# Longformer attention and a cosine MLP on one core: values through a padded ring in DRAM, global rows through a scratch, and two waits fewer in the opening order

## The chip, the cores and the metric

One core of a Trainium2 chip runs the whole program. The metric is device time in microseconds (us). A core has a matrix engine (TensorE, PE; loading of its weights is shown as PEld), a vector engine (DVE), a scalar engine (ACT), GpSimd (POOL) and a sync engine (SP). Each takes its own instructions in order and waits on semaphores for the others. DMAs are issued here by SP (plain copies and transposes) and by POOL (copies that change the type, and indirect gathers); both kinds run on the same 16 DMA engines, from two queues (q1 for SP's, q0 for POOL's).

## The reference, cut to what matters

```python
# q, k, v: (8, 8, 576, 64) fp32; global_idx: 8 sorted positions
scores = scale * np.matmul(q, k.transpose(0, 1, 3, 2))
mask = np.abs(pos[:, None] - pos[None, :]) <= 32
mask = mask | is_global[:, None] | is_global[None, :]
scores = np.where(mask, scores, -1e9)
attn = np.exp(scores - scores.max(-1)) / (sum + 1e-9)
x = np.matmul(attn, v)            # then (8 * 576, 512): heads side by side
h = x @ w_in                      # 512 -> 2048
out = (h * np.cos(h)) @ w_out     # 2048 -> 512
```

## The kernel before

The 64 heads are worked in 32 **pairs** (two heads of one batch element); two pairs, four heads, are a **half** (16 halves, numbered like the steps s). A head's 576 rows are cut into 12 blocks of 48 queries. A block sees 112 keys (its 48 and 32 on either side) and the 8 global keys: KW = 120 rows. Before row 0 the window is filled with the head's own last 32 rows (KL = 32), after the last row with any finite rows; the mask takes out what does not count. The global queries ride as 8 extra columns in every block.

For one pair `pr` the steps are:
- `local_k`, `local_q` (k, q in the order strings): keys and queries of the blocks into `kw` and `qb`. Up to pair 7 they come from `kn`, `qn` (loaded by POOL, `load_qk`) and PE turns them; ACT copies, and L419, a small POOL copy, puts the last 32 keys in front. From pair 8 on they come from `kT`, `qT`, which SP loads with DMA transposes (`turn_half`, L262, L263) out of the fp16 copies `k16`, `q16` in DRAM; DVE copies (L423 to L437).
- `globals_kq` (g): POOL copies the global columns into `kw`, `qb` (L393 to L398).
- `scores` (s): 12 matmuls `st` (L447), ACT's exp (L449), DVE's mask (L450).
- `values` (p): 24 matmuls `pv` (L458) with the value tile `vw[pr % 4]`; DVE divides by the sums into `xn` (L463 to L469). `p5` is this step for pair 5.
- `turn_x` (x): PE turns `xn` (L481), DVE writes `xT` (L484); after a batch element's last pair POOL writes its 8 global rows (L489).

**Values.** `cast_half` with "v" (L246) has POOL copy four heads of v to fp16 in DRAM, `v16`, one array for all heads. `load_v` fills a pair's `vw` tile from it with four SP DMAs, or five for odd pairs: block 0 apart, its wrapped 32 rows apart, blocks 1 to 11 per head, and for odd pairs the last block of the second head apart. `load_vg` (L309) adds the 8 global value rows per head from `vgw`, an SBUF tile that `spread_globals` (ACT, L379) writes every eight pairs from the gathered rows `vg32`. Every window row is a run of 64 fp16, 128 bytes.

**Global rows.** For every eight pairs POOL gathers the global rows of k, q and v (L284); ACT copies k's and q's (`copy_globals`, L368), PE turns them (`turn_globals`, L373).

**MLP.** `mlp_in` (one, "1"): four matmuls `ph` (L497), ACT's cosine (L500), DVE's product (L501). `mlp_out` (two, "2"): four matmuls `po` (L511). They fill PE between attention steps as far as whole batch elements are ready. From pair 32 on only the MLP is left.

**Order.** The order is written out by hand: each engine runs its instructions in the order in which the code issues them. Pairs 0 to 3 and what feeds later ones follow the string `FRONT`; then a loop over s = 2 to 15 runs `THIRD` (s = 2) or `ORDER`, with scores of pair 2s (`sa`) and 2s+1 (`sz`), their values (`pa`, `pz`), and local keys for the next step (`kc` to `qd`). `G` calls `casts(s)`: POOL waits for pair 2s+1's `xn` with a small copy into `gate` (L680), then in s = 2, 6 and 10 gathers the next global rows, and casts a half of v, k, q (in s = 4 two). In the same steps `b` calls `copy_globals`, `t` `turn_globals` and `spread_globals`. At the end of a step SP issues `turn_half(s + 2)` and the loads of pairs 2s+4 and 2s+5.

In `FRONT`, besides the letters above: `I` loads the indices into POOL registers; `W0` to `W3` and `O0` to `O3` are POOL loads of quarters of w_in and w_out with a change of type; `L2` loads k and q of half 2 into `kn`, `qn`; `c2` casts v of half 2; `v4` is `load_values(4)` on SP; `n` a sum of squares on ACT. `w3` makes POOL wait until pair 3's values have landed, by a one-element copy out of `vw` (L660); `w5` and `w7` do the same for pairs 5 and 7. Everything that POOL has behind such a step in its order waits with it.

Of the kernel before, what the change touches and what calls it, by code (L numbers as in the profile page):

```python
# [10 lines left out]
FP16 = mybir.dt.float16  # L11
# [6 lines left out]
B, H, S, D = 8, 8, 576, 64  # L18
NT, DM, DFF = 4608, 512, 2048
P = 128  # L20
NP = H // 2
QB = 48
NB = 12
G = 8
W = 112
KW = G + W
BP = 6
GP = 8
KL = 32
# [11 lines left out]

THIRD = "sa0 sa1 sa2 sz0 sz1 sz2 1 pa 1 xa pz G 1 1 kc qc xz 1 1 b kd qd 1 n t 1"

FRONT = ("g0 k1 q1 s0.0 s0.1 s0.2 g1 s1.0 s1.1 s1.2 g2 g3 k2 q2 p0 s2.0 s2.1 s2.2 k3 q3 p1 x0 s3.0 s3.1 s3.2 I w3 W0 L2 W1 c2 c3 "
         "p2 x1 p3 x2 x3 g4 g5 v4 v5 1 1 k4 q4 w5 W2 L3 W3 1 1 k5 q5 n0 1 1 v6 v7 g6 g7 w7 O0 O1 O2 O3")
OK_ALL = float(P * (B * NP * 2 * BP + B))


def view(ap, *dims):

    return bass.AP(ap.tensor, ap.offset, [ap.ap[0], *[list(d) for d in dims]])


def dview(ap, offset, *dims):

    return bass.AP(ap.tensor, ap.offset + offset, [list(d) for d in dims])
# [134 lines left out]
def kernel(  # L191
# [10 lines left out]
    nc = tc.nc  # L202
# [3 lines left out]
    dram = ctx.enter_context(tc.tile_pool(name="dram", bufs=1, space=bass.MemoryType.DRAM))  # L206
# [18 lines left out]

    q16 = dram.tile([2 * B, S, 4 * D], FP16)
    k16 = dram.tile([2 * B, S, 4 * D], FP16)
    v16 = dram.tile([B * H * S, D], FP16)


    NV = 4
# [4 lines left out]
    vw = [keep.tile([P, 2, NB, D + 1], FP16, name=f"vw{i}") for i in range(NV)]  # L236
# [4 lines left out]
    def cast_half(s, which):  # L241

        base = s * 4 * S * D
        for x in which:
            if x == "v":
                nc.gpsimd.dma_start(v16[s * 4 * S : (s + 1) * 4 * S].rearrange("(n r) d -> n (r d)", r=16),  # L246
                                    dview(v, base, (16 * D, 4 * S // 16), (1, 16 * D)))
            else:
                src, dst = {"k": (k, k16), "q": (q, q16)}[x]
                nc.gpsimd.dma_start(dst[s].rearrange("t (h d) -> t h d", h=4),  # L250
                                    dview(src, base, (D, S), (S * D, 4), (1, D)))
# [8 lines left out]
    def turn_half(s):  # L260

        nc.sync.dma_start(kT[s % 2][:, :, KL : KL + S], k16[s], transpose=True)  # L262
        nc.sync.dma_start(qT[s % 2], q16[s], transpose=True)  # L263
# [24 lines left out]


    vgw = keep.tile([P, NB, D + 1], FP16)  # L290

    def load_v(pr):


        vt, n0, p0 = vw[pr % NV], 2 * pr * S * D, G + KL
        nc.sync.dma_start(vt[p0:KW, :, 0, 0:D], dview(v16, n0, (D, W - KL), (S * D, 2), (1, D)))
        nc.sync.dma_start(vt[G:p0, :, 0, 0:D], dview(v16, n0 + (S - KL) * D, (D, KL), (S * D, 2), (1, D)))
        for h in range(2):
            lo, i1 = n0 + (h * S - KL) * D, NB
            if pr % 2 and h:  # L300

                i1 = NB - 1
                nc.sync.dma_start(vt[G : KW - KL, h, i1, 0:D], dview(v16, lo + QB * i1 * D, (D, W - KL), (1, D)))  # L303
            nc.sync.dma_start(vt[G:KW, h, 1:i1, 0:D], dview(v16, lo + QB * D, (D, W), (QB * D, i1 - 1), (1, D)))

    def load_vg(pr):
        for h in range(2):
            p0 = (pr % GP * 2 + h) * G
            nc.sync.dma_start(vw[pr % NV][0:G, h], vgw[p0 : p0 + G])  # L309


    mask = keep.tile([KW, NB, 2, C], FP16)
# [52 lines left out]
    def copy_globals(which):  # L365
        for x in which:
            g16 = g16_of[x] = work.tile([P, 2, D], FP16, tag="g16", name="g16")
            nc.scalar.copy(g16, view({"k": kg32, "q": qg32}[x], (0, 2), (1, D)))  # L368

    def turn_globals(which, n):  # L370
        for x in which:
            t = ps.tile([P, GP, 2, G], FP16, tag="s", bufs=3)
            nc.tensor.transpose(t.rearrange("x n h g -> x (n h g)"), g16_of.pop(x).rearrange("x h d -> x (h d)"), ident16)  # L373
            for h in range(2):
                hp = slice(h * D, (h + 1) * D)
                nc.scalar.copy({"k": kgT, "q": qgT}[x][hp, GP * n : GP * (n + 1)], t[hp, :, h])

    def spread_globals():
        nc.scalar.copy(vgw[:, :, 0:D], view(vg32, (0, NB), (1, D)))  # L379


    w_in16 = const.tile([P, NC, DFF], FP16)
# [143 lines left out]
    def x_squares(s):  # L526

        sq = work.tile([P, 2 * BP * P], FP16, tag="sq", bufs=1)
        xn = xn_of.pop(s)
        nc.scalar.activation(sq, view(xn, (1, 2 * BP * P)), AF.Square,  # L530
                             accum_out=x_sq[:, s : s + 1])
# [47 lines left out]
    def one(n=1):  # L579
        for _ in range(n):  # L580

            if ins_q and ins_q[0][0] < ready[0] and ins_q[0][0] < outs_q[0][0] + 2:
                t, f = ins_q.pop(0)
                mlp_in(t, f)
                ready[1] = t * NF + f + 1

    def two(n=1):
        for _ in range(n):
            t, u = outs_q[0] if outs_q else (NTT, 0)

            need = min(t * NF + 4 * (u % 4) + 12, NTT * NF) if tail[0] else min(t * NF + 4 * (u % 4) + 7, (t + 1) * NF)
            if outs_q and need <= ready[1] and (tail[0] or NTT * NF - len(outs_q) < outs_by[0]):
                mlp_out(*outs_q.pop(0))
# [7 lines left out]
    with tc.manual_schedule():  # L601
# [16 lines left out]
        nc.gpsimd.iota(d_i, pattern=[[-1, C]], base=0, channel_multiplier=1)  # L618
        index_rows()
        for i in range(NV):  # L620
            if i % 2:
                nc.vector.memset(vw[i][:, 1, NB - 1], 0.0)
            nc.vector.memset(vw[i][:, :, :, D : D + 1], 1.0)
        gather(k, kg32, 0)
        gather(q, qg32, 0)
        cast_half(0, "v")
        cast_half(1, "v")
        gather(v, vg32, 0)
        load_qk(1)
# [7 lines left out]
        local_q(0)  # L637
        nc.vector.memset(view(pv[:, :, D : D + 1], (512, 2), (65, 6)), 1.0)
        load_v(0)
        spread_globals()  # L640
        load_vg(0)
        for pr in (1, 2, 3):
            load_v(pr)
            load_vg(pr)

        def load_w_in(c):
            nc.gpsimd.dma_start(w_in16[:, :, c * 512 : (c + 1) * 512],
                                moe_w_in[:, c * 512 : (c + 1) * 512].rearrange("(c p) n -> p c n", p=P))
# [5 lines left out]
        def load_values(pr):  # L654
            load_v(pr)
            load_vg(pr)
# [17 lines left out]
        def globals_kq(pr):  # L674
            globals_k(pr)
            globals_q(pr)

        def casts(s):

            nc.gpsimd.tensor_copy(gate[0:1], xn_of[s][0:1, 1, 0, 0:1])  # L680
            if s % 4 == 2 and s // 4 < 3:
                for src, dst in ((k, kg32), (q, qg32), (v, vg32)):
                    gather(src, dst, s // 4 + 1)
            for n in range(4, 2 * B):
                if s == (n - 2 if n < 7 else n - 3):
                    cast_half(n, "vkq")
# [4 lines left out]
                 "I": load_idx, "O": load_w_out, "w": wait_values, "1": units}  # L691
        for step in FRONT.split():
            f = (STEPS | OTHER)[step[0]]
# [5 lines left out]
        for s in range(2, B * NP // 2):  # L699
            outs_by[0] = 4 * (s - 2) if s < 5 else 8 * (s - 3)  # L700
            for pr in (2 * s + 2, 2 * s + 3):
                if 8 <= pr < B * NP:
                    globals_kq(pr)
            for step in (THIRD if s == 2 else ORDER).split():
                if step == "1":
                    one()
                elif step == "2":
                    two()
                elif step == "n":
                    x_squares(s - 1)  # L710
                elif step == "G":
                    casts(s)
                elif step in "bt":

                    if s % 4 == 2 and s // 4 < 3:
                        if step == "b":
                            copy_globals("kq")
                        else:
                            turn_globals("kq", s // 4 + 1)
                            spread_globals()  # L720
                else:
                    f, pr = (STEPS | LOCAL)[step[0]], 2 * s + "azcd".index(step[1])
                    if pr < B * NP:
                        f(pr, *[int(x) for x in step[2:]])
            if s % 2 == 1:
                ready[0] = s // 2 + 1 + (s // 2 == B - 1)
            if s < B * NP // 2 - 2:
                turn_half(s + 2)
                load_values(2 * s + 4)
                load_values(2 * s + 5)  # L730
# [49 lines left out]
```

## Time and profile before

| | us |
|---|---|
| median of three runs (lowest, highest) | 413.0 (410.2, 416.48) |
| the profiled execution | 410.63 |
| its span, first to last instruction | 408.9 |
| PE busy, share of the span | 332.7, 81% |
| DVE, ACT, POOL busy | 258.2, 248.7, 120.1 |
| DMA q0 (POOL's): packets, MB | 64,000, 18.75 |
| DMA q1 (SP's): packets, MB | 122,722, 28.28 |
| mean granted TensorE clock | 0.948 |

Times in the text are from the span's start, in the profiled execution. A row of the chain of waits gives a start, a length and what the end of the program was waiting on then. "A <- B" in the list of waits means that A stood until B was done: total us, times, longest. The trace also holds a record of every DMA packet with its queue, size, start and length; it doesn't say on which of the 16 engines a packet ran.

### The profile page before, as it was taken

What the parts mean: (1) busy time and instruction counts of PE and PEld (TensorE: products, weight loads), DVE (VectorE), ACT (ScalarE), POOL (GpSimd) and SP (SyncE); (2) the same over time, 40 slices, a digit from 0 to 9 for tenths busy, and PEclk for the clock granted to TensorE, in tenths of its full rate; (3) what the DMA queues carried; (4) which work ended last, traced back from release to release, by engine and by line L of the source; (5) the groups of instructions that cost most, each with busy time, mean ns of one, the idle gap of its engine ahead of it and who ended that gap; (6) DMA issues with size and microseconds to landing.
All of it is one profiled execution on the core that took longest, in us unless ns stands there. A gap on an engine that the chain in (4) does not pass through costs nothing.

```text
span 408.9 us, 7734 instructions
## 1 busy us (share of the span) xinstructions
PE 332.7 (81%) x2778; PEld 178.7 (44%) x2778; DVE 258.2 (63%) x606; ACT 248.7 (61%) x380; POOL 120.1 (29%) x264
## 2 busy tenths in 40 slices
PE   0573909219497999699999999999999979999993
PEld 0562404105243554355555545555555424444441
DVE  4764427205958878588887898878888544634300
ACT  7760746129457776677678786777767866344310
POOL 7405131641609254433507265250200100000000
PEclk9999977757799999899999999999999999999999
DMA  6957989599999998999999999999841000010121
GB/s 97 139 72 109 160 105 177 83 199 118 125 118 173 124 172 158 162 139 188 109 190 149 156 153 144 199 140 157 163 79 54 26 0 27 26 53 26 52 79 59
DMA packets 186767, 47.60 MB, mean 116 GB/s; under 512 B 174754, under 2 KB 181666, under 8 KB 186466
## 3 DMA queue, kind: packets, MB, share of 16 engines
q0 software_dynamic: 64000, 18.75, 47.1%
q1 hardware_dynamic: 122722, 28.28, 43.8%
q8 instruction: 24, 0.39, 0.4%
q14 instruction: 21, 0.17, 0.1%
HBM read 48.05 MB, written 21.23 MB: 169 GB/s over the span
## 4 chain that ended last, share of the span: by engine, by line
PE 64%; DMA 11%; ACT 8%; issue 4%; DVE 4%; SPq 3%; POOL 3%; POOLq 0%; ACTq 0%; DVEq 0%
PE po L511 27%; PE ph L497 26%; DMA vw<-v 5%; PE st L447 4%; DMA kg<-in_k_dram,gidx_rows 4%; PE pv L458 3%; PE tx L481 2%; ACT cos L500 2%; DVE g L501 2%; SPq L309 1%; SPq L303 1%; ACT e L449 1%; ACT L449 1%; ACT sq L530 1%; POOL xT L489 1%
## 5 line engine op out<-in xcount | busy, mean ns | idle before, releaser
L497 PE MATMUL ph<-xT,w_in 128*128 128x512 f16 x576 | 144.4, 388 | 9.7 <-DVE g L501 6.2
L500 ACT ACTIVATE cos<-ph,pio 128x512 f16<-128x512 f32 x144 | 97.0, 686 | 77.6 <-PE ph L497 77.3
L511 PE MATMUL po<-w_out,g 128*128 128x512 f16 x576 | 142.6, 385 | 0.0
L501 DVE TENSOR_TENSOR g<-cos,ph 128x512 f16<-128x512 f16 x144 | 96.9, 686 | 62.2 <-ACT cos L500 60.1
L497 PEld LDWEIGHTS <-w_in 128*128 128x128 f16 x576 | 54.1, 99 | 72.2 <-issue 14.4
L511 PEld LDWEIGHTS <-g 128*128 128x128 f16 x576 | 56.0, 100 | 63.6 <-issue 3.1
L449 ACT ACTIVATE e<-st 120x448 f16<-120x448 f32 x96 | 46.3, 545 | 27.4 <-PE st L447 24.6
L450 DVE TENSOR_TENSOR pm<-e,mask 120x448 f16<-120x448 f16 x96 | 37.3, 395 | 28.1 <-ACT e L449 25.4
L447 PE MATMUL st<-qb,kw 128*120 128x112 f16 x384 | 33.3, 239 | 23.6 <-POOL kw L419 9.6
L447 PEld LDWEIGHTS <-kw 128*120 128x120 f16 x384 | 32.2, 154 | 33.5 <-POOL kw L419 10.5
L680 POOL COPY gate<-xn 1x1 f16<-1x1 f16 x14 | 2.5, 179 | 133.2 <-DVE xn L469 133.2
L469 DVE TENSOR_TENSOR xn<-pv,r_all 128x768 f16<-128x768 f32 x32 | 30.7, 958 | 1.9
L250 POOL DMA_DIRECT2D q<-in_q_dram x12 | 27.2, 2264 | 0.0
L516 ACT COPY o<-po 128x512 f32<-128x512 f32 x18 | 10.5, 584 | 22.2 <-PE po L511 22.0
L530 ACT ACTIVATE sq<-xn 128x1536 f16<-128x1536 f16 x16 | 23.6, 1474 | 0.0
L434 DVE COPY qb<-t 64x576 f16<-64x576 f16 x10 | 7.6, 758 | 24.8 <-ACT qb L434 23.0
L489 POOL COPY xT<-xg 128x4 f16 x64 | 21.1, 329 | 6.9 <-DVE xT L484 3.5
L458 PE MATMUL pv<-vw,pm 120*56 120x65 f16 x768 | 20.3, 204 | 2.8 <-DVE xT L484 2.2
L250 POOL DMA_DIRECT2D k<-in_k_dram x12 | 21.1, 1756 | 0.0
L481 PE MATMUL tx<-ident,xn 128*128 128x128 f16 x192 | 17.3, 231 | 4.6 <-DVE xn L469 2.5
L518 DVE COPY o<-po 128x512 f32<-128x512 f32 x18 | 12.3, 685 | 12.7 <-PE po L511 12.7
L500 ACT ACT_TABLE_LOAD x15 | 19.2, 1283 | 0.3
(107 smaller groups left out, 286.1 us busy)
## 6 DMA issues: line engine op xcount, KB each, us to landing
out_dram<-o SPq DMA_DIRECT2D x36, 256.0 KB
vw<-v SPq DMA_DIRECT2D x48, 154.0 KB
v<-in_v_dram POOLq DMA_DIRECT2D x16, 288.0 KB, 5.1
k<-in_k_dram POOLq DMA_DIRECT2D x12, 288.0 KB, 8.1
q<-in_q_dram POOLq DMA_DIRECT2D x12, 288.0 KB, 10.4
vw<-v SPq DMA_DIRECT2D x16, 140.0 KB
w_in<-in_moe_w_in_dram POOLq DMA_DIRECT2D x4, 512.0 KB, 8.2
w_out<-in_moe_w_out_dram POOLq DMA_DIRECT2D x4, 512.0 KB, 9.2
```

What stands on the lines that cost most here:

```text
L250: nc.gpsimd.dma_start(dst[s].rearrange("t (h d) -> t h d", h=4), dview(src, base, (D, S), (S * D, 4), (1, D)))
L447: nc.tensor.matmul(st[:, j], kp[:, 4 * g + j], view(qp[:, 4 * g + j], (1, 2 * C)), start=True, stop=True)
L449: nc.scalar.activation(e, st, AF.Exp, scale=scale)
L450: nc.vector.tensor_tensor(view(pm[:, 4 * g], (1, n)), view(e, (1, n)), view(mask[:, 4 * g], (1, n)), ALU.mult)
L458: nc.tensor.matmul(pv[r0 : r0 + C, j // 6, c0 : c0 + 65], pm[:, j, h], vp[0:KW, h, j], start=True, stop=True)
L469: nc.vector.tensor_tensor(view(xn, (384, 2), (D, 6), (1, D)), view(pv, (512, 2), (65, 6), (1, D)), view(rp, (6, 2), (1, 6), (0, D)), ALU.mult)
L481: nc.tensor.transpose(tx[:, n], xn[:, n], ident16)
L497: nc.tensor.matmul(ph, w_in16[:, j, f * P : (f + 1) * P], xT[:, j, t * TT : (t + 1) * TT], start=(j == 0), stop=(j == NC - 1))
L500: nc.scalar.activation(cos, ph, AF.Sin, bias=pio2)
L501: nc.vector.tensor_tensor(g16[:, f], cos, ph, ALU.mult)
L511: nc.tensor.matmul(po, g16[:, f, s * P : (s + 1) * P], w_out16[:, f], start=(f == 0), stop=(f == NF - 1))
L530: nc.scalar.activation(sq, view(xn, (1, 2 * BP * P)), AF.Square, accum_out=x_sq[:, s : s + 1])
```

## The change

- `v16` becomes a ring of four buffers, one per half. In a buffer each head has 32 + 576 rows: its last 32 rows, then all its rows; 32 more rows close the buffer. A half is cast by two POOL DMAs: one for the heads' rows (4 heads x 4 runs), one for the last rows of the four heads and of the next one (5 runs).
- A head's windows are then one regular pattern, so `load_v` is two SP DMAs a pair, 112 partitions x 12 blocks x 64 each. The memsets of a block of odd tiles go.
- `spread_globals(n)` also has SP write `vgw` to a scratch in DRAM, `vgs[n % 2]`. `load_vg` takes both heads' rows from there in one DMA; pairs 0 and 1 still take them from `vgw`.
- The first loads are issued in another order: each pair's global rows stand ahead of the next pair's values.
- In `FRONT`, `w5` and `w7` go; `W2` moves up behind `c2`; `W3`, `L3` and `c3` move behind `g4 g5 v4 v5 1 1`; `O0` to `O3` follow `g7` at once.

```diff
-FRONT = ("... I w3 W0 L2 W1 c2 c3 "
-         "p2 x1 p3 x2 x3 g4 g5 v4 v5 1 1 k4 q4 w5 W2 L3 W3 1 1 k5 q5 n0 1 1 v6 v7 g6 g7 w7 O0 O1 O2 O3")
+FRONT = ("... I w3 W0 L2 W1 c2 W2 "
+         "p2 x1 p3 x2 x3 g4 g5 v4 v5 1 1 W3 L3 c3 k4 q4 1 1 k5 q5 n0 1 1 v6 v7 g6 g7 O0 O1 O2 O3")
...
-    v16 = dram.tile([B * H * S, D], FP16)
+    VB = 4
+    VR = (KL + S) * D
+    v16 = [dram.tile([4 * (KL + S) + KL, D], FP16, name=f"v16_{i}") for i in range(VB)]
...
             if x == "v":
-                nc.gpsimd.dma_start(v16[s * 4 * S : (s + 1) * 4 * S].rearrange("(n r) d -> n (r d)", r=16),
-                                    dview(v, base, (16 * D, 4 * S // 16), (1, 16 * D)))
+                part = S * D // 4
+                nc.gpsimd.dma_start(dview(v16[s % VB], KL * D, (VR, 4), (part, 4), (1, part)),
+                                    dview(v, base, (S * D, 4), (part, 4), (1, part)))
+                n = 5 if s < 2 * B - 1 else 4
+                nc.gpsimd.dma_start(dview(v16[s % VB], 0, (VR, n), (1, KL * D)),
+                                    dview(v, base + (S - KL) * D, (S * D, n), (1, KL * D)))
...
     vgw = keep.tile([P, NB, D + 1], FP16)
+    VH = NB * (D + 1)
+    vgs = [dram.tile([P, VH], FP16, name=f"vgs{i}") for i in range(2)]

     def load_v(pr):
-        vt, n0, p0 = vw[pr % NV], 2 * pr * S * D, G + KL
-        nc.sync.dma_start(vt[p0:KW, :, 0, 0:D], dview(v16, n0, (D, W - KL), (S * D, 2), (1, D)))
-        nc.sync.dma_start(vt[G:p0, :, 0, 0:D], dview(v16, n0 + (S - KL) * D, (D, KL), (S * D, 2), (1, D)))
         for h in range(2):
-            lo, i1 = n0 + (h * S - KL) * D, NB
-            if pr % 2 and h:
-                i1 = NB - 1
-                nc.sync.dma_start(vt[G : KW - KL, h, i1, 0:D], dview(v16, lo + QB * i1 * D, (D, W - KL), (1, D)))
-            nc.sync.dma_start(vt[G:KW, h, 1:i1, 0:D], dview(v16, lo + QB * D, (D, W), (QB * D, i1 - 1), (1, D)))
+            nc.sync.dma_start(vw[pr % NV][G:KW, h, :, 0:D],
+                              dview(v16[pr // 2 % VB], (2 * (pr % 2) + h) * VR, (D, W), (QB * D, NB), (1, D)))

     def load_vg(pr):
-        for h in range(2):
-            p0 = (pr % GP * 2 + h) * G
-            nc.sync.dma_start(vw[pr % NV][0:G, h], vgw[p0 : p0 + G])
+        p0 = pr % GP * 2 * G
+        if pr < 2:
+            for h in range(2):
+                nc.sync.dma_start(vw[pr % NV][0:G, h], vgw[p0 + h * G : p0 + (h + 1) * G])
+        else:
+            nc.sync.dma_start(vw[pr % NV][0:G].rearrange("g h n d -> g h (n d)"),
+                              dview(vgs[pr // GP % 2], p0 * VH, (VH, G), (G * VH, 2), (1, VH)))
...
-    def spread_globals():
+    def spread_globals(n):
         nc.scalar.copy(vgw[:, :, 0:D], view(vg32, (0, NB), (1, D)))
+        nc.sync.dma_start(vgs[n % 2], vgw.rearrange("x n d -> x (n d)"))
...
         load_v(0)
-        spread_globals()
-        load_vg(0)
-        for pr in (1, 2, 3):
-            load_v(pr)
+        spread_globals(0)
+        for pr in range(4):
             load_vg(pr)
+            if pr < 3:
+                load_v(pr + 1)
```

More of the change, by code (lines that the diff above doesn't have):

```diff
@@ L42 @@
 THIRD = "sa0 sa1 sa2 sz0 sz1 sz2 1 pa 1 xa pz G 1 1 kc qc xz 1 1 b kd qd 1 n t 1"
-FRONT = ("g0 k1 q1 s0.0 s0.1 s0.2 g1 s1.0 s1.1 s1.2 g2 g3 k2 q2 p0 s2.0 s2.1 s2.2 k3 q3 p1 x0 s3.0 s3.1 s3.2 I w3 W0 L2 W1 c2 c3 "
-         "p2 x1 p3 x2 x3 g4 g5 v4 v5 1 1 k4 q4 w5 W2 L3 W3 1 1 k5 q5 n0 1 1 v6 v7 g6 g7 w7 O0 O1 O2 O3")
+FRONT = ("g0 k1 q1 s0.0 s0.1 s0.2 g1 s1.0 s1.1 s1.2 g2 g3 k2 q2 p0 s2.0 s2.1 s2.2 k3 q3 p1 x0 s3.0 s3.1 s3.2 I w3 W0 L2 W1 c2 W2 "
+         "p2 x1 p3 x2 x3 g4 g5 v4 v5 1 1 W3 L3 c3 k4 q4 1 1 k5 q5 n0 1 1 v6 v7 g6 g7 O0 O1 O2 O3")
 OK_ALL = float(P * (B * NP * 2 * BP + B))
@@ L620 @@
         for i in range(NV):
-            if i % 2:
-                nc.vector.memset(vw[i][:, 1, NB - 1], 0.0)
             nc.vector.memset(vw[i][:, :, :, D : D + 1], 1.0)
@@ L719 @@
                             turn_globals("kq", s // 4 + 1)
-                            spread_globals()
+                            spread_globals(s // 4 + 1)
                 else:
```

## The prediction

> **What bounds the kernel now.** I read the page's slices first.
>
> ```profile
> PE   0573909219497999699999999999999979999993
> PEclk9999977757799999899999999999999999999999
> DMA  6957989599999998999999999999841000010121
> ```
>
> A slice is 10.2 us. From slice 13 on TensorE (PE) is nearly always busy and DMA is dense without stopping it; the holes are in the first 130 us, above all in slices 5 and 7 to 8. Busy time by stage sizes them (columns: stretch, length, then busy time and count of PE, PEld, DVE, ACT, POOL; clock, DMA share, GB/s):
>
> ```profile
> 51.00:61.00 10.00, 0.44 (x6) 0.31 (x5) 2.69 (x8) 4.24 (x8) 3.76 (x8) 0.73 0.83 102
> 75.50:92.00 16.50, 1.40 (x6) 0.70 (x6) 0.56 (x1) 2.89 (x7) 10.03 (x14) 0.52 1.28 174
> 164.00:172.00 8.00, 4.87 (x34) 2.69 (x35) 4.43 (x7) 5.28 (x12) 3.96 (x8) 0.98 1.23 149
> 172.00:235.00 63.00, 63.00 (x552) 34.48 (x551) 51.81 (x125) 46.77 (x70) 23.03 (x49) 0.98 1.38 154
> ```
>
> So PE stands 9.6 us, then 15.1 us, then 3.1 us (length less PE's busy time); 172 to 235 is full. A microsecond taken out of the front reaches the end, since what follows is PE work of fixed order. Which wait ends last in the holes, the chain of waits says (start, us, what):
>
> ```profile
> 53.50 3.26 DMA vw<-v
> ...
> 56.88 0.18 POOL gate L660
> ...
> 60.45 0.21 POOL kw L419
> ...
> 60.70 1.46 PE st L447 x12
> ...
> 63.69 10.32 DMA vw<-v
> ...
> 74.14 0.18 POOL gate L660
> ...
> 78.50 10.50 DMA kg<-in_k_dram,gidx_rows
> ```
>
> Hole one: `w5` holds POOL until pair 5's values land; three weight and input loads and pair 5's small key copy (L419) are queued behind it, and PE needs that copy. Hole two: `w7` holds POOL to 74.14; w_out's four loads go out just ahead of the second gather of global rows, which therefore lands after 10.5 us; ACT needs it at 89.0. Hole three, from the waits:
>
> ```profile
> POOL gate L660 <- DMA vw<-v: 28.7, 3, 11.7
> ACT vgw L379 <- DMA out_dram<-o: 2.6, 1, 2.6
> ```
>
> The second line is ACT at 167.92. The stores named had not been a reader of vgw; the two vw<-vgw loads issued at 163.1 to 164.4 are, and vgw can't be overwritten before they land.
>
> **Part 1, the loads of values (SP).** Before: 2 x 0.44 (L296, L297) + 2 x 0.42 (L304) + 2 x 0.64 (L309) = 3.0 us a pair by medians, 0.57 more for odd pairs. After: 2 x 0.42 + 0.64 = 1.5. The 128-byte packets stay (85,504 before; 32 x 2,688 = 86,016 after), so it is issue time only. It counts where SP is the limit: for the first four pairs SP issues from 13.15 to 31.85, and `w3` passes at 33.67. After: eight loads at about 0.5 and six or seven global-row loads and one scratch write at 0.65 are 9 us from 13.15, plus the wait for ACT's vgw (ends 15.57) that was there before: SP ends near 23.5 and the values land near 26. POOL reaches `w3` at 26.8 (after the L419 of 26.57). `w3` at 27.0: 6.7 earlier. On PE only 0.5 comes of it (p2 waits for that load from 29.46 to 30.05, then DVE and PE alternate to 40.65).
>
> **Part 2, the casts.** One POOL DMA becomes two: +0.52 us (L246's median) of POOL a half. Two of them now stand ahead of the first gather of v, for which ACT waits at 14.72 already: up to +1.0. In s=3 (POOL chain 105.15 to 110.41) +0.5. Elsewhere covered: in s=5 the eight xT copies end at 147.45 and the first new `ph` runs at 152.28, 4.8 us of cover for 0.5. The scratch ring of four halves costs no wait: half n overwrites half n-4, loaded over 17 us earlier. How long the data takes is unknown: the packet records show each old cast as 16 packets of 18,432 bytes at 1.58 us (median). Bounds: all 16 beside each other, 1.6, or all in a row, 25. The pieces have the same size as the old ones, so I take 1.6. [...] Four at a time is a rival below.
>
> **Part 3, two POOL waits less.** W0 goes out at 27.0; v4's loads followed W0 by 13.3 us before (34.17 to 47.45, when c2 had landed), so they start at 40.3. Pair 5's L419 follows ACT L417 (ends 49.39), so its scores start near 51.2, not 60.70: -9.5. But what is late next is the data of pairs 4 and 5. W2, W3, L3, c3 now share the 16 DMA engines with them, and w_out follows at 51.5 (k5's L419, then g6, g7 at 1.9). Count from 41.3, by the packet records (512 packets of 1,024 bytes for a quarter of w_in or w_out, 576 for k and q of a half): what is left of W2, about 250, + 512 + 576 + 4 x 512 = 3,390 large packets plus one cast, against 2 x 2,688 = 5,376 of 128 bytes. Where both queues ran before (63 to 69 us) the records show 956 and 1,087: 160 a us and 1.14 to 1. So the large ones take 21 us, with the cast until 64; 3,860 small ones went with them, 1,500 follow at 1,100 a us (30 to 31 us): 65.4, and p5 at 66. If the small ones got nothing until the end, the large ones would run at 200 a us (37 to 39 us) and end at 60, and the small ones at 65: the order hardly matters. Earliest p5: 51.2 + 6.77 (60.70 to 67.47 before) = 58. Latest: 76, if `w3` passes no earlier and mixed traffic is slower still (the large packets' 98 ns were 130 at 66 us). I take 66, 1.5 before the old 67.47.
>
> The gate of s=2 then passes at p5 + 2.2 (end of xn) = 68.2, since w7 is gone and w_out has landed; gather 0.34 later, landing 5.2 (median): 73.7. PE's work after p5 lasted 8.07 before (to 75.54), so to 74.1: the rows are there, and the 13.5 us from 75.54 to 89.02 go. Together -15.0.
>
> **Part 4, vgw through a scratch.** Four more SP DMAs, between 0.36 (an out store's issue) and 0.66 (L309) each, taken at 0.66; the write waits for ACT's vgw. Behind it on SP stand turn_half and the next loads; in s=2 and s=6 these wait for k16 or for earlier issues anyway. load_vg(2) needs the scratch landed: written at 16.3, asked at about 21. vgw is free once the write has read it, so the 2.6 us at 167.92 go. The gap at 238 is 0.4; nothing is counted for it.
>
> **Sum.** -15.0 - 2.6 + (1.0 - 0.5) + 0.5 = -16.6. The profiled execution took 410.6 (span 408.9): 394.0. The median of the runs shown is 413.0, 2.4 above it: 396.
>
> **Rivals.** *Better:* small packets go first, p5 at 58, the gather lands behind w_out at 66 to 70: about -22 in place of -15, 389. For: the engines had free stretches around 47 to 58 us. Against: 63 to 69 us, where they shared.
>
> *Casts four pieces at a time:* 6.3 us for 1.6. The first two, side by side, end 3.1 later (before: 3.2 together); ACT's vgw and the whole front move by that, 0.5 of it not counted twice: +2.6. In s=4 the cast of k lands up to 4.7 later; q's transposes ended at 143.3 and DVE reads them at 145: 1.7 of slack, +3.0. That is +5.6: 402. For: the new pattern's outer count is 4. Against: 16 equal pieces as before. [...]
>
> *Late values:* p5 at 76 gives back 10: 406. For: two L309 took 5.2 us at 64.28 beside weight loads. Against: the packet count above ends at 65 in either order.
>
> *Slower:* the second DMA of a cast writes between the rows of the first; if it is ordered behind it, POOL stands until the first has landed. Price: 6.4 us each for c0 and c1 (6.77 to 13.15) before the gather of v: +12.8; c2 lands 10.3 after POOL reaches it, which holds the xT copies by 1.3; c3, behind W3 and L3, 8.4, which holds k4's copy by 6.5. That is 20.6 in the front: p5 at 79 to 87, say 83, and s=3 begins 11.7 later at 94.7, 2.0 later than now. s=3 loses 5.6 (5.1 landing, 0.5 issue), six odd steps 0.8 each (5.6 less 4.8 of cover), and 2.6 are gained: about +10, with the 2.4: 423. It decides once the holds in the front exceed 15 us in sum. Against: L296 and L304 write into each other's range of vw in the same way, and L304 was issued at 14.01 while L296, of 13.15, was under way. That is SBUF; no such pair in DRAM is in this trace.
>
> **How the numbers follow.** Forecast 0.48, better 0.08, four at a time 0.20, late values 0.10, POOL held 0.14. Two per cent, 8.3 us, is about what a measurement can tell. Faster (under 404.7): 0.47 + 0.08 + 0.14 + 0.04 = 0.73; within: 0.01 + 0.06 + 0.06 + 0.03 = 0.16; slower 0.11. The range 387 to 409 takes in all but the last rival and edges. The forecast's own is 391 to 402 (p5 from 61 to 72).
>
> **What would show it.** Right: w3's gate near 27; PE's hole at 51 to 61 replaced by one that ends at p4 or p5 on DMA vw<-v16; p5 near 66; ACT's wait for kg gone or short; s=3's first `st` near 78, not 92.7; no wait at L379 in s=6; 172 to 235 still full. Wrong: packets of the cast in fours, k16 late at SP in s=3 and s=4; POOL standing between the two DMAs of a cast; PE holes after 130 us that end on kT or vw.

## The result, and the profile after

| | before | after |
|---|---|---|
| median, us (lowest to highest; 4 runs each) | 411.6 (408.39 to 416.48) | 427.47 (425.41 to 429.74) |
| the profiled execution; its span | 410.63; 408.9 | 425.51; 423.6 |

The ratio of the times is 1.041, with a 95% interval of 1.030 to 1.053: the change made the kernel slower by some 16 us, where 16.6 us less was forecast. Ratios here and below are taken over the executions in the faster of two states and medians over all, so a ratio isn't always the quotient of the medians beside it. The slices (10.6 us each, in tenths) show that this isn't one new hole:

```profile
PE   0364831967848898998996989898999988998994
PEclk9999985898988999999998899998999999999998
DMA  5985999999999999999999999999991000010021
```

Before, PE stood at 9 in all slices from 13 to 31 but one. Now there are 8s and a 6 up to slice 27, and the granted clock falls to 0.8 in slices 21, 22 and 27 (0.87 in 222.4 to 233 us, 0.81 in 233 to 243.6, 0.83 in 286 to 296), while DMA stays dense. The same stretches as before (length, then busy time and count of PE, PEld, DVE, ACT, POOL; clock, DMA share, GB/s) give the sizes:

```profile
51.00:61.00 10.00, 5.34 (x35) 3.06 (x33) 5.00 (x14) 9.50 (x16) 5.10 (x13) 0.83 1.32 193
61.00:75.50 14.50, 2.81 (x29) 1.41 (x30) 1.83 (x5) 0.00 (x0) 0.00 (x0) 0.57 1.13 168
75.50:92.00 16.50, 12.16 (x147) 6.84 (x147) 8.62 (x17) 13.37 (x24) 9.58 (x16) 0.97 1.02 93
...
172.00:235.00 63.00, 56.98 (x488) 30.58 (x487) 49.23 (x113) 42.32 (x63) 23.26 (x49) 0.96 1.38 141
235.00:300.00 65.00, 60.32 (x503) 31.53 (x501) 51.22 (x114) 43.50 (x68) 24.78 (x45) 0.96 1.37 150
```

Two of the old front holes shrank: 51 to 61 has 5.3 us of PE work where it had 0.4, and 75.5 to 92 has 12.2 where it had 1.4. A new one of 11.7 us stands from 61 to 75.5, on the values of pairs 4 and 5. And the stretch from 172 to 300, which was full (63.0 and 64.4 us of PE work before), now lacks 6.0 and 4.7 us. Before, the second of these was:

```profile
235.00:300.00 65.00, 64.36 (x572) 35.03 (x571) 55.30 (x132) 49.39 (x79) 23.46 (x53) 1.00 1.29 156
```

The list of waits names what the front hole and part of the rest waited for (total us, times, longest):

```profile
PE pv L466 <- DMA vw<-vgs: 13.2, 2, 9.6
...
PE pv L466 <- DMA vw<-v: 11.0, 7, 3.4
...
ACT vgw L386 <- DMA vg<-in_v_dram,gidx_rows: 4.4, 1, 4.4
```

PE's wait for a value tile, which before was once 0.3 us, has become a standing one. The chain of waits (start, us, what) has these transfers both in the front and late in the program:

```profile
52.27 20.60 DMA vw<-v
...
72.92 0.87 PE pv L466 x23
...
129.89 10.16 DMA vw<-v
...
264.02 11.17 DMA vw<-v
...
278.75 12.05 DMA vw<-v
```

The next table compares when scores and values start with the kernel before, in us (minus is earlier); s12 is the scores of pair 12, p20 the values of pair 20. The forecast's row puts the terms of its sum where they belong in the program.

| | p5 | s=3's first st | s of pair 8 | s12 | s16 | p20 | s26 | end |
|---|---|---|---|---|---|---|---|---|
| after | +8.7 | -4.9 | -7.0 | +1.8 | -1.1 | +5.4 | +10.9 | +14.7 |
| forecast | -1.5 | -14.5 | -14.0 | -14.0 | -16.6 | -16.6 | -16.6 | -16.6 |

So the waits that were removed did bring the program forward, by 7.0 us at pair 8. From there to the end 21.7 us were lost, in a part in which the forecast moved nothing but the 2.6 us of pair 14. PE's waits for values between 130 and 330 us make up 11.0 of these. One more hole, of 5.51 us, stands at 126.86 ahead of the scores of pair 10 (e1, below: 1.85): POOL's copy of global queries, behind the casts of two halves, and DVE's copy of q, which stood 3.89 us for q's transpose, end within 0.2 us of each other there. The rest isn't traced to single waits.

What the loads waited behind shows in the DMA issues (KB each, median us from issue to landing):

```profile
v<-in_v_dram POOLq DMA_DIRECT2D x16, 288.0 KB, 9.2
k<-in_k_dram POOLq DMA_DIRECT2D x12, 288.0 KB, 12.2
q<-in_q_dram POOLq DMA_DIRECT2D x12, 288.0 KB, 17.6
```

Before:

```profile
v<-in_v_dram POOLq DMA_DIRECT2D x16, 288.0 KB, 5.1
k<-in_k_dram POOLq DMA_DIRECT2D x12, 288.0 KB, 8.1
q<-in_q_dram POOLq DMA_DIRECT2D x12, 288.0 KB, 10.4
```

The casts of k and q weren't touched by the change, and they land 4.1 and 7.2 us later. The packet records say how a cast of v now runs: 12 packets of 24,576 bytes, which start four at a time in three rounds (half 2's at about 45, 47 and 49 us). Before it was 16 packets of 18,432 bytes, up to 16 of them beginning together.

### The profile page after: what moved, and what is told of

Same layout as the page of the kernel before. It is cut to its first block, busy times and chain, and to the rows that moved or that the text cites. A ratio compares the mean times of both kernels' runs of the same rounds, so it can differ in the third digit from the quotient of the medians.

```text
span 423.6 us, 7631 instructions
## 1 busy us (share of the span) xinstructions
PE 339.0 (80%) x2778; PEld 179.4 (42%) x2778; DVE 264.1 (62%) x604; ACT 249.4 (59%) x380; POOL 131.7 (31%) x278
## 4 chain that ended last, share of the span: by engine, by line
PE 36%; issue 21%; DMA 20%; POOL 13%; ACT 5%; POOLq 1%; DVE 1%; SPq 0%; ACTq 0%; DVEq 0%
PE ph L505 16%; PE po L519 16%; DMA vw<-v 13%; POOL q L258 3%; DMA vg<-in_v_dram,gidx_rows 3%; DMA kT<-k 2%; POOL xT L497 2%; PE pv L466 2%; ACT cos L508 1%; PE st L455 1%; POOL v L250 1%; POOL k L258 1%; POOL v L254 1%; DMA qg<-in_q_dram,gidx_rows 1%; ACT kw L422 1%
## 5 line engine op out<-in xcount | busy, mean ns | idle before, releaser
L505 PE MATMUL ph<-xT,w_in 128*128 128x512 f16 x576 | 148.1, 395 | 10.5 <-DVE g L509 5.8
L519 PE MATMUL po<-w_out,g 128*128 128x512 f16 x576 | 144.3, 388 | 0.0
L509 DVE TENSOR_TENSOR g<-cos,ph 128x512 f16<-128x512 f16 x144 | 97.4, 686 | 67.3 <-ACT cos L508 64.4
L455 PE MATMUL st<-qb,kw 128*120 128x112 f16 x384 | 32.4, 234 | 22.3 <-ACT e L457 5.5
L455 PEld LDWEIGHTS <-kw 128*120 128x120 f16 x384 | 30.8, 149 | 32.9 <-issue 12.2
L466 PE MATMUL pv<-vw,pm 120*56 120x65 f16 x768 | 21.6, 206 | 25.5 <-DMA vw<-vgs 13.2
L466 PEld LDWEIGHTS <-pm 120*56 120x56 f16 x768 | 17.5, 116 | 29.6 <-issue 27.2
L524 ACT COPY o<-po 128x512 f32<-128x512 f32 x18 | 10.5, 584 | 22.2 <-PE po L519 22.0
L432 DVE COPY kw<-kT 128x1344 f16<-128x1344 f16 x24 | 20.7, 861 | 0.6
## 6 DMA issues: line engine op xcount, KB each, us to landing
k<-in_k_dram POOLq DMA_DIRECT2D x12, 288.0 KB, 12.2
q<-in_q_dram POOLq DMA_DIRECT2D x12, 288.0 KB, 17.6
```

What stands on the lines that cost most here:

```text
L455: nc.tensor.matmul(st[:, j], kp[:, 4 * g + j], view(qp[:, 4 * g + j], (1, 2 * C)), start=True, stop=True)
L466: nc.tensor.matmul(pv[r0 : r0 + C, j // 6, c0 : c0 + 65], pm[:, j, h], vp[0:KW, h, j], start=True, stop=True)
L505: nc.tensor.matmul(ph, w_in16[:, j, f * P : (f + 1) * P], xT[:, j, t * TT : (t + 1) * TT], start=(j == 0), stop=(j == NC - 1))
L509: nc.vector.tensor_tensor(g16[:, f], cos, ph, ALU.mult)
L519: nc.tensor.matmul(po, g16[:, f, s * P : (s + 1) * P], w_out16[:, f], start=(f == 0), stop=(f == NF - 1))
```

## The experiments

The theory after this profile: the outermost count of the new large cast (the count of the slowest loop of its two access patterns) is 4, and four of its packets start at a time; so few DMA engines carry its data, and the transfers that follow are as late as those few. That few engines carry it was the author's guess: no record names one. Rivals: the new order of the front (weights, w_out and values at once), the fact that there are two casts for one, or the two-DMA loads and the scratch.

**e1: both casts written with 16 outermost.** The same bytes go to the same places. The loop over runs is now the outermost one, and has 16 short runs where it had 4 (large cast) or 1 (small cast). The new order, the two casts, the two-DMA loads and the scratch all stay.

```diff
-                part = S * D // 4
-                nc.gpsimd.dma_start(dview(v16[s % VB], KL * D, (VR, 4), (part, 4), (1, part)),
-                                    dview(v, base, (S * D, 4), (part, 4), (1, part)))
+                part = S * D // 16
+                nc.gpsimd.dma_start(dview(v16[s % VB], KL * D, (part, 16), (VR, 4), (1, part)),
+                                    dview(v, base, (part, 16), (S * D, 4), (1, part)))
...
-                nc.gpsimd.dma_start(dview(v16[s % VB], 0, (VR, n), (1, KL * D)),
-                                    dview(v, base + (S - KL) * D, (S * D, n), (1, KL * D)))
+                run = KL * D // 16
+                nc.gpsimd.dma_start(dview(v16[s % VB], 0, (run, 16), (VR, n), (1, run)),
+                                    dview(v, base + (S - KL) * D, (run, 16), (S * D, n), (1, run)))
```

> The changed kernel, but both DMAs of a cast have 16 runs as their outermost count (16 runs of 2,304 values by 4 heads; 16 runs of 128 values by 5), the same bytes to the same places. Theory A (the cast goes four pieces at a time, and the few DMA engines that carry it make every later DMA late): cast packets start 16 together, the value loads of pairs 20, 21, 26 and 27 land in time, and the 16 us that are lost from pair 19 (1.5 ahead of before) to the end (14.7 behind) go; time 400 to 408 us, ratio to before 0.97 to 0.99. Theory B (the two waits taken from POOL cost it, by loads of weights ahead of loads of values): p5 stays near 76 us and the ratio stays at 1.03 to 1.05.

Measured: 396.02 us, 0.9645 of the kernel before (0.9592 to 0.9699), whose median beside it was 410.23; theory A had asked for 400 to 408. The DMA issues and two of the stretches of e1:

```profile
v<-in_v_dram POOLq DMA_DIRECT2D x16, 288.0 KB, 5.2
k<-in_k_dram POOLq DMA_DIRECT2D x12, 288.0 KB, 7.4
q<-in_q_dram POOLq DMA_DIRECT2D x12, 288.0 KB, 10.5
```

```profile
172.00:235.00 63.00, 62.01 (x559) 33.41 (x558) 55.47 (x124) 48.51 (x77) 28.02 (x59) 1.00 1.45 160
235.00:300.00 65.00, 64.80 (x553) 35.07 (x552) 54.82 (x130) 48.60 (x73) 18.10 (x46) 1.00 1.25 140
```

All three landings are back within 0.1 us of the old ones or below, and the steady part is full again. Against before, e1 is 12.4 us early at pair 8 and 12.4 early at the end of its profiled execution: what the front gains, it keeps. There is no wait of PE for values in 130 to 330; in after that stretch held 11.0 us of them (7.5 on v, 3.5 on the scratch).

**e2: only the new order**, put on the kernel before.

```diff
-FRONT = ("... I w3 W0 L2 W1 c2 c3 "
-         "p2 x1 p3 x2 x3 g4 g5 v4 v5 1 1 k4 q4 w5 W2 L3 W3 1 1 k5 q5 n0 1 1 v6 v7 g6 g7 w7 O0 O1 O2 O3")
+FRONT = ("... I w3 W0 L2 W1 c2 W2 "
+         "p2 x1 p3 x2 x3 g4 g5 v4 v5 1 1 W3 L3 c3 k4 q4 1 1 k5 q5 n0 1 1 v6 v7 g6 g7 O0 O1 O2 O3")
```

> The kernel before with the new opening order alone (w5 and w7 gone, W2, W3, L3, c3 moved); casts, value loads and global rows as before. Theory A: no steady loss; p5 at 66 to 72, the gather of global rows no longer behind w_out, 396 to 404 us, ratio 0.96 to 0.985. Theory B: ratio 1.02 to 1.05, with p5 at 74 or later.

**e3: the old order**, put on after (the two strings of e2 the other way about).

> The changed kernel with the opening order of before (w5 and w7 back). Theory A: front back at s=3 near 93 to 96 us, the loss in the steady part stays or grows: 425 to 435 us, ratio 1.03 to 1.06. Theory B: 405 to 412 us, ratio 0.985 to 1.0 (the wait for vgw in s=6 is gone).

**e4: the old order with the wide casts of e1.**

> The changed kernel with both: casts with 16 runs outermost, and the opening order of before. Theory A: what is left of the change is fewer SP DMAs and the scratch of global rows, so 405 to 411 us, ratio 0.985 to 1.0, s=3 beginning at 90 to 93 us. Theory B: the same as with the old order alone, within 1 per cent.

The four against the kernel before, and after for comparison:

| loads and casts | old order | new order |
|---|---|---|
| old | 1 | e2: 402.4 us, 0.976 (0.971 to 0.982) |
| new, wide casts | e4: 403.01, 0.984 (0.979 to 0.989) | e1: 396.02, 0.9645 (0.959 to 0.970) |
| new, narrow casts | e3: 425.31, 1.032 (1.025 to 1.038) | after: 427.47, 1.041 (1.030 to 1.053) |

The order is worth 2.4% by itself and 2.0% with the wide casts, so it isn't what made the kernel slower. With the narrow casts it is worth nothing (1.032 and 1.041, intervals that overlap). The new loads with wide casts are worth 1.6% without the order. Between the second row and the third lie 4.8% in the one order and 7.7% in the other: the narrow casts are the cause, and they cost more in the new order. Theory A's ranges held for e2 and e3; e4 came out 2 us under its own.

**f1: of e1, only the large cast back at 4 outermost; f2: only the small one back at 5; f3: the large one at 8.**

```diff
-                part = S * D // 16
-                nc.gpsimd.dma_start(dview(v16[s % VB], KL * D, (part, 16), (VR, 4), (1, part)),
-                                    dview(v, base, (part, 16), (S * D, 4), (1, part)))
+                part = S * D // 8
+                nc.gpsimd.dma_start(dview(v16[s % VB], KL * D, (part, 8), (VR, 4), (1, part)),
+                                    dview(v, base, (part, 8), (S * D, 4), (1, part)))
```

(f3; f1 and f2 put one statement each of after back.)

> The wide-cast kernel with the first DMA of a cast (288 KB) back at 4 as its outermost count, the second left at 16. Theory A1 (the large DMA on few engines is the whole loss): cast packets 4 at a time, value loads late again, ratio to before 1.02 to 1.05, about 425 us. Theory A2 (the small second DMA, 5 outermost, does harm of its own, since it is what the loads of the first blocks wait for): ratio 0.97 to 1.0. Theory A3 (only the size of the pieces matters, 24,576 against 4,608 bytes) says the same here as A1.

> The wide-cast kernel with the second DMA of a cast (20 KB) back at 5 as its outermost count, the first left at 16. Theory A1: within 1 per cent of the wide-cast kernel, ratio 0.96 to 0.975. Theory A2: ratio 0.985 to 1.03.

> The wide-cast kernel with the first DMA of a cast at 8 as its outermost count (8 runs of 4,608 values by 4 heads: 32 pieces of 9,216 bytes). If the number of engines that carry the cast decides, packets start 8 at a time, a cast takes twice as long as with 16, and the time lies between the two: ratio 0.965 to 1.0. If the piece size decides, it is near the wide-cast kernel, under 0.97, and the number that start together does not matter.

Measured beside a kernel before of 412.42: f1 426.78 us, 1.034 (1.029 to 1.040); f2 398.72, 0.967 (0.962 to 0.971); f3 405.58, 0.983 (0.978 to 0.989). The large cast alone brings back 7.0% of the 7.7% between e1 and after; the small one can't be told from nothing. Eight outermost lies between. The packet records of the large cast line up with it:

| outermost | packets of a cast | most that begin together | first start to last end, median us | landing of v, k, q, us | time to before |
|---|---|---|---|---|---|
| 16 runs (before) | 16 of 18,432 B | 16 | 3.0 | 5.1, 8.1, 10.4 | 1 |
| 4 heads (after) | 12 of 24,576 B | 4 | 5.9 | 9.2, 12.2, 17.6 | 1.041 |
| 4 heads (f1) | 12 of 24,576 B | 4 | 6.0 | 9.2, 12.6, 15.0 | 1.034 |
| 8 (f3) | 32 of 9,216 B | 8 | 4.0 | 6.1, 9.6, 12.5 | 0.983 |
| 16 (e1) | 64 of 4,608 B | 16 | 2.6 | 5.2, 7.4, 10.5 | 0.9645 |

A cast's packets take about the same time when added up (12 x 1.86 = 22 us in after, 64 x 0.36 = 23 in e1), so it isn't more work, only less of it side by side. The size of the packets moves along with the outermost count in f1, f3 and e1, and no run varies it alone. Size by itself doesn't fit the table: before, with 18,432 bytes and 16 outermost, v, k and q landed sooner (5.1, 8.1, 10.4) than in f3 with 9,216 and 8 (6.1, 9.6, 12.5). The starts come in 4, 8 and 16 as the outer count does; how many engines a cast used isn't shown.

**f4 and g1: can the front gain more?** In e1 the values of pairs 4 and 5 still run beside w_out's loads. f4 puts w_out's four loads behind the gathers of s=2. g1 sends half 2's cast right after W0, O0 and O1 after those gathers, and O2 and O3 after the casts of s=2.

```diff
 # f4
-         "... k5 q5 n0 1 1 v6 v7 g6 g7 O0 O1 O2 O3")
+         "... k5 q5 n0 1 1 v6 v7 g6 g7")
...
+            if s == 2:
+                for c in range(4):
+                    load_w_out(c)
 # g1
-FRONT = ("... I w3 W0 L2 W1 c2 W2 "
+FRONT = ("... I w3 W0 c2 L2 W1 W2 "
...
```

> The wide-cast kernel with the four loads of w_out issued in s=2 behind the gathers of global rows, not in the opening order. If pairs 4 and 5 wait for their values because those share the engines with w_out (50 to 66 us in the wide-cast kernel), p5 comes at 58 to 62 us and not at 71.4, s=3 begins at 70 to 76 and not at 83, and the time is 385 to 392 us, ratio 0.94 to 0.957. If the loads are late by W2, W3, L3 and c3 alone, or w_out now holds up the casts of half 4, p5 stays over 66 or the gain is given back by s=4: ratio 0.96 to 0.98.

> The wide-cast kernel with c2 issued right behind W0, two loads of w_out behind the gathers of s=2 and the other two behind its casts. If the front is bound by when c2 has landed and by what runs beside the loads of pairs 4 and 5, SP starts these at 42 to 45 us and not at 46.9, p5 comes at 57 to 62, s=3 begins at 72 to 77, and with the casts of half 4 no longer behind all of w_out the lead holds: 386 to 393 us, ratio 0.94 to 0.955. If the small packets stay at about 190 a us beside W2, W3, L3 and c3 whatever their start, p5 stays at 62 to 65 and the ratio at 0.96 to 0.97.

Measured: f4 397.81 us, 0.9645 (0.960 to 0.969); g1 396.06, 0.968 (0.957 to 0.978). Neither can be told from e1. Both miss the range that was hoped for (385 to 392 and 386 to 393 us). In g1 pair 5's values start at 61.2. In f4 they start at 63.3 (e1 71.4) and s=3 is 14.7 us early (e1 9.7), but at pair 8 it is 12.6 early and e1 12.4. PE's timeline of f4 shows where the 5 us went (start, us, engine, line, operation; in brackets the idle time before and what ended it):

```profile
97.81 1.42 PE L456 MATMUL st<-qb,kw 128*120 128x112 f16 x12 [7.26 <-POOL kw L402]
```

Ahead of that copy of global keys POOL has the gate of s=3, which passes at 90.05 when pair 7's `xn` is there, the casts behind it (90.62 to 95.0) and 3.29 us of copies of xT. DVE's copy of q, which stood 1.51 us for its transpose, ends as late (97.71). In g1 the hole is 4.96 us, at 95.67, on POOL's copies of xT. So an earlier front meets the work that starts only behind the gate; that moving this work would gain the 5 us wasn't tried.

**g2: e1 without the scratch of global rows** (`load_vg` reads `vgw` as before, two DMAs a pair).

```diff
-        if pr < 2:
+        if True:
...
-        nc.sync.dma_start(vgs[n % 2], vgw.rearrange("x n d -> x (n d)"))
```

> The wide-cast kernel without the scratch of global rows: the global rows of every pair come from vgw by two SP DMAs, as before, and nothing is written to DRAM. By the sum the scratch is worth the wait for vgw in s=6, 2.6 to 3.7 us: this kernel 0.6 to 1.0 per cent slower than the wide-cast kernel, ratio 0.970 to 0.977, with a hole at the scores of pair 15. If the scratch's write in the opening (3.5 us of SP, behind it the first global rows) costs as much as it saves, ratio 0.96 to 0.97; p0 and p1 come 1 to 2 us earlier here in either case.

Measured: 397.47 us, 0.968 (0.959 to 0.976). The wait that the scratch was forecast to remove is back, in the list of waits of g2 for 150 to 180 us:

```profile
ACT vgw L383 <- DMA out_dram<-o: 2.3, 1, 2.3
```

But the time differs from e1's by 0.3%, inside both intervals. The wait costs PE nothing: pair 14's values start at 160.90 in g2 and at 160.88 in e1. The scratch's first write stands in SP's opening for 3.47 us in e1, and the values of pairs 0 and 1 start 0.6 and 1.1 us later than in g2 (1.7 and 1.6 later than before), but by pair 8's scores e1 and g2 are 0.1 apart.

The best version is e1: 396.02 us, faster than both kernels. f4 and g1 equal it.

## Why the prediction was wrong

**The step that failed is Part 2's data time:** "The pieces have the same size as the old ones, so I take 1.6." The pieces don't (24,576 bytes, not 18,432: the four runs of a head are one stretch of memory, and it was cut in three), and size by itself doesn't fit the table above. Four of them begin at a time, in three rounds, and a cast takes 5.9 us where 3.0 were usual. The sum also has no term for what a cast does to the transfers beside and behind it, and that was the larger part. The 31 us between e1 and after hang on how the casts are written, and f1 puts 7.0 of 7.7% on the large cast alone.

With the casts put right, the total comes close to the forecast: e1 is 14.2 us under its own before (410.23 to 396.02) where 16.6 were forecast. That is partly luck, since the parts differ. At s=3 e1 is 9.7 early and not the 15.0 of Part 3, by an error in Part 1 (below). From there to pair 8 it gains 2.8 more, where a loss of 0.5 was forecast: PE's hole ahead of pair 8's scores was 4.75 us before and is 1.95. Part 4's 2.6 aren't there.

**The rival with the right mechanism had the wrong price.** "Casts four pieces at a time" was given 402 us and 0.20. It counted the landing of the cast itself, in the front and before q's transposes of s=4: 5.6 us. Its ground, the outer count of 4, rested on no comparison of counts when it was written: every cast of v in before has 16 runs outermost, with up to 16 packets beginning together. It is f1, f3 and e1 that show starts in 4, 8 and 16 for counts of 4, 8 and 16. And it left out what a cast does to other transfers. While half 2's packets ran in after, the 1,024-byte packets of POOL's loads went out at about 150 a us where 200 were usual. At 68 to 72 us w_out's last packets ran at 122, 95, 82 and 26 a us. At 110 to 115 us the 128-byte packets of the k and q casts ran at 125 to 284 a us, nearly alone, where before reached 1,207 and e1 1,192. The author's estimate from the first pair of rates is that four engines of 16 were busy with the cast (150 of 200 is what the other 12 would move) and that the transfers beside it ended late by their share on those four. The records don't name engines, so this is not shown; that the loss goes when the outermost count is 16 is shown (1.034 in f1, 0.9645 in e1). SP suffers by it too. Its timeline in after (start, us, engine, line, operation) has loads of values standing at issue:

```profile
54.01 5.93 SPq L315 DMA_DIRECT2D vw<-vgs  x1
60.04 12.08 SPq L306 DMA_DIRECT2D vw<-v  x2
...
281.28 8.26 SPq L306 DMA_DIRECT2D vw<-v  x2
```

Such a pair of loads, forecast at 0.42 us each, takes 12.08 and 8.26 (in e1, at the same place in the front, 8.61). After 100 us the longest two take 4.42 in e1, 9.19 in after. What stands behind them on SP stands too, and PE sees it late in the program as in the front:

```profile
72.92 0.87 PE L466 MATMUL pv<-vw,pm 120*56 120x65 f16 x23 [3.41 <-DMA vw<-v]
...
290.84 0.56 PE L466 MATMUL pv<-vw,pm 120*56 120x65 f16 x23 [1.88 <-DMA vw<-v]
```

The steady part's DMA slices stood at 9, so a late transfer had little room to catch up; this is argued, not tested. The forecast's own words, "172 to 235 is full", were read as "nothing is lost there"; they also say that nothing can be late there for free. The rival's 5.6 us, worked out from landings alone, were under a fifth of the 31 us between e1 and after.

**Part 1** was wrong in its time for `w3`, in two ways. "POOL reaches `w3` at 26.8" forgot the step `I` between: eight register loads of the indices, 5.3 us. And "the values land near 26" was too early: in e1 SP issues pair 3's last load of values at 26.71, behind the scratch's write of 3.47 us among others, and its data lands at 32.73. POOL's timeline in after, where the register loads end last:

```profile
35.45 0.18 POOL L666 COPY gate<-vw 1x1 f16<-1x1 f16 x1 [5.21 <-issue]
```

The loads fill 30.0 to 35.3. Before, they ran from 26.55 to 31.85 and were hidden under a wait of 6.89 us for pair 3's values. In e1 they run from 26.76 to 32.07, the values land 0.7 us later, and the gate passes at 32.85, 0.8 us earlier than before, where 6.7 were forecast. In after the gate is later by another 2.6. One part of that is the first gather of v, which lands behind the first casts: ACT starts `vgw` at 17.84 where it was 14.72, and the list of waits has the 4.4 us. "Up to +1.0" was allowed for it.

**Part 3** was right in its kind. The two waits are gone, the hole that follows ends on the values, as listed, and the second gather is no longer behind w_out. Its size was too good: v4's loads begin at 51.87 in after and 46.89 in e1 (40.3 forecast). In e1 that is 13.5 us behind W0, as forecast (13.3), so `w3` alone makes them late; in after it is 15.9, with the cast late too. Pair 5's values start at 76.2 and 71.4 (66 forecast), and s=3 is 4.9 and 9.7 us early (15.0 by Part 3). The count of packets took 1.14 small ones to a large one. In e1 both went at about 190 a us (57 to 65 us), and in after 100 small to 190 large (60 to 67 us), so that the values came last. Of the other rivals "late values" has its p5 of 76 in after, and its condition, that `w3` passes no earlier, nearly held. Of the 10 us beyond 66, e1 shows 4.8 as a consequence of the narrow cast; the other 5.4 are in e1 too, with the late `w3`.

**Part 4** was right that the wait at vgw in s=6 would go, and wrong in what that is worth. Pair 14's values follow its scores 3.8 us sooner than before in after and 3.7 in e1, but nothing of it reaches the values: in e1 the scores start at 155.19 and the values at 160.88, and in g2, which has the wait, at 153.17 and 160.90.

**"POOL held"** is out: the two casts follow each other on POOL without a gap (6.79 and 7.48 us, each under 0.7 long). Its 423 us came close to the time measured, by another mechanism. The places tell them apart: that rival had s=3 begin 2.0 us later than before, and it is 4.9 earlier; the loss comes behind pair 8, most of what is traced of it on values.

Of the signs listed for "wrong", three appeared: packets in fours, holes after 130 us that end on vw, and k16 late at SP (in s=3 the transposes of k go out 11.8 us after k's cast, against 6.9 before and 6.6 in e1).

## What to carry to other kernels

Where a DMA is rewritten, compare the outermost count of its patterns with the old one before anything else. Here the large cast had the same 288 KB and nearly the same issue time (0.63 us, 0.52 before), while its packets began four at a time where up to 16 had; putting 16 runs outermost in one statement was worth some 29 us (f1 to e1). Where DMA is dense, price such a transfer by what else is in flight, not by who reads it: the untouched casts of k and q landed 4 and 7 us later. And when a long wait is taken away, list what its engine does in that time, since that work can be the next limit: 5.3 us of register loads here.

## What was not expected of the hardware

- A contiguous row of 73,728 bytes (fp16) was cut into three packets of 24,576, though the pattern asked for four runs of 18,432. With the loop over runs outermost (e1, f3) each run stayed a packet of its own.
- Between 4 and 16 outermost the time didn't go evenly: 1.034, 0.983, 0.9645. Going from 4 to 8 recovers 5.1 of the 7.0%; the packets get smaller along with it.
- Small and large packets of the two queues shared by count in e1: 185 large and 187 small a us at 57 to 65 us. In after it was 188 to 103 (60 to 67 us). Why the shares are even in one and not in the other isn't shown.
- POOL stands ahead of a DMA as well: 2.43 us ahead of w_out's last quarter (58.58 us, after), until one of w_in's loads landed. Why that issue needed the landing isn't shown.
